# A retention and SwiGLU kernel: the first 740 of its listed steps in another order

## The chip, the cores and the metric

The kernel runs on one core of one Trainium2 chip. The metric is the device time of one execution in microseconds (us). Five engines work side by side, each in the order of its own program: TensorE (PE; its weight loads, PEld, are listed apart), VectorE (DVE), ScalarE (ACT), GpSimd (POOL) and SyncE (SP), which here only starts transfers (DMAs).

## The reference

Two blocks follow one another, all in float32. The first is a recurrent retention over 768 positions for 4 batches and 8 heads of 64 columns. The second is a SwiGLU feed-forward block on its result.

```python
gamma = 1.0 - 2.0 ** (-5.0 - np.arange(H))          # B, H, S, D = 4, 8, 768, 64
for t in range(S):
    state = gamma[None, :, None, None] * state + np.einsum('bhd,bhe->bhde', k[:, :, t], v[:, :, t])
    y[:, :, t] = 1.0 / np.sqrt(D) * np.einsum('bhd,bhde->bhe', q[:, :, t], state)
x = y.transpose(0, 2, 1, 3).reshape(3072, 512)
g = x @ w_gate                                       # 512 x 1536
val = x @ w_val                                      # 512 x 1536
out = (g / (1 + np.exp(-g)) * val) @ w_out           # 1536 x 512
```

## The kernel before

*Products.* A float32 operand of a large product is split into three terms of the shorter type fp32r, and three (or, for two split operands, several) products are summed in a PSUM bank. The first term is a rounding by ScalarE (lines 1129, 1138), the second a remainder by VectorE (lines 418, 1132), the third a remainder by GpSimd (lines 1135, 1141) or VectorE (line 1145). So every operand passes through three engines before TensorE can use it.

*Tiling.* The 3072 tokens are taken in four segments of 768 tokens, six chunks of 128 each. A segment has an up stage (gate and value products for 12 blocks `f` of 128 of the 1536 columns, silu, product of the two) and a down stage (`D`: for each `f` and each of the six chunks, three matmuls into one of six banks). The up stages of segments 1 to 3 use a scheme with seven products per block (line 1230). The retention of the next segment runs between the steps of the down stage.

*Order.* The string `PLAN` lists the names of all steps; `run()` goes through it and executes each step, so that each engine's instructions, and the transfers in SyncE's queue, stand in the order of the list.

```python
for key in PLAN.split():
    if key in events:
        events.pop(key)[2]()
    else:
        do(key)
```

A step can hold work of one engine or a transfer, and an engine does its steps strictly in that order, whichever of them is ready first. A transfer is issued by SyncE in list order and, before it is issued, waits for its target buffer to be free.

*Names of steps in segment 0.* A name is a letter, a number and, after the colon, a part.

- `A` loads parts of the decay tables; `l c:0` to `l c:3` load chunk `c` (keys, queries, values and the keys in rows: four transfers of 256 KB); `P` loads the chunks' data for segment 1 (line 928).
- `s c` scores (matmuls L651, masked by VectorE L657); `m c` mix of the scores with the values (L742); `o` the part of the older state (L728); `t` the new state (matmuls L713, VectorE L718); `r` transposes keys (L692); `k` and `q` scale keys and queries on GpSimd, `K` and `Q` on VectorE, `E` on ScalarE; `g` lets a state decay (ScalarE), `I` makes a unit matrix.
- `x c:0` to `x c:2` split a chunk's result into three terms: `x4:1` is the remainder term of chunk 4 (VectorE L418).
- `U`, `V` bring a weight block's raw 64-bit words; `a`, `b`, `c` (ScalarE L553, L556, L559), `S` and `C` (VectorE L566, L574; GpSimd L576 for the blocks 12 to 17 of the down weights) turn them into float32; `T` makes sums and differences of weight terms for the scheme of the later segments (VectorE L418); `Z` stores the converted weights for the later segments; `n f:0` to `n f:5` make the three terms of gate and value weights.
- `p f:j` and `v f:j`, for `f` = 0 and 1, are the gate and value products for two of the six chunks (L1075, 12 matmuls of 256 columns each); `G f:i` and `W f:i`, for `f` from 2, are those products for three chunks (L1057); `u`/`i` is the silu, `y`/`j` the product of the two (VectorE L1086, L463).

*Names in the down stage and in the retention of segment 1.* `0/W f` loads a block of the down weights and `0/d f.0` to `0/d f.2` split it (ScalarE L1138, GpSimd L1141, VectorE L1145). `0/h f.0` to `0/h f.2` split the block's activations. `0/D f.tok` are the three matmuls for one chunk of tokens (L1301). `1/sc p` are scores (matmuls L825), `1/dec p.i` masks them (VectorE L956), `1/q`, `1/k` scale queries and keys, `1/A p`, `1/B p` and `1/C p` are three mixes (matmuls L825), `1/y...` copies of their results, `1/x...` splits of the sum. `0/e` and `0/o` end a chunk's output and store it.

`down` of line 1295 shows what a `D` step asks of the others:

```python
for n, (g, a) in enumerate(own):
    nc.tensor.matmul(o, hs[g][:, a, ds(i * TH + u * P, P)], wo[g][:, a, cols],
                     start=n == 0 and (f == 0 or final),
                     stop=f == NF - 1 and a == 2, skip_group_check=True)
```

The three matmuls read the terms `a` = 0, 1, 2 of the activations `hs` (steps `0/h`) and of the weights `wo` (steps `0/d`), one after the other, and `o` is a bank that another product may still hold.

Of the kernel before, what the change touches and what calls it, by code (L numbers as in the profile page):

```python
# [25 lines left out]
L = 3  # L26
# [65 lines left out]
    0/D2.5 1/sc1 0/D2.0 0/d4.0 1/was1.0 0/D2.4 0/d4.1 0/D3.4 1/l6 1/dec1.1 0/h5.2 1/dec1.0 0/D2.2
    1/x0.2.0 0/D3.1 1/q1.1 0/d4.2 0/W5 0/D3.5 1/x0.1.0 0/h6.0 1/k1.0 0/Z3 1/sum0.3 1/k1.1 1/sum0.2
    1/x0.2.1 0/D4.5 0/D3.2 0/D3.3 0/D3.0 1/q1.0 0/Z4 0/h6.1 0/D4.0 0/D4.4 1/x0.1.2 1/x0.1.1 1/A1
    1/x0.0.0 0/d5.0 1/x0.2.2 1/y1.00 0/h6.2 1/y1.06 1/x0.0.2 1/new1.0 0/D4.2 0/d5.1 0/d5.2 0/D4.3 0/D4.1
    1/y1.07 1/y1.01 0/W6 0/h7.0 1/B1 1/x0.0.1 1/y1.04 1/y1.12 0/h7.1 1/l9 0/d6.0 0/D5.4 0/h8.0
    0/d6.1 1/y1.02 0/D5.3 0/D5.2 0/W7 0/h8.1 1/y1.05 0/d6.2 1/l8 1/l11 0/Z5 1/y1.03 1/was1.1
# [30 lines left out]
    1/p8.4 1/w9.0.1 2/l1 0/o5 0/o4 1/u5.7 2/k0.0 2/cv3 1/u7.8 1/w9.1.2 1/w9.0.2 1/L11 2/l0
    1/u7.9 1/p9.0 1/u8.1 1/w8.2.2 1/u8.5 1/u8.6 1/p9.1 1/w10.1.0 1/w10.2.0 1/w10.0.0 1/u9.0 1/u7.2 1/w9.2.1
    1/w10.1.1 1/w10.1.2 1/w10.0.1 2/l4 1/w10.0.2 1/p9.3 1/p9.2 1/u9.4 1/p8.6 1/u9.3 1/p9.4 1/p9.5 1/u8.2  # L130
    1/u8.8 1/u8.9 1/p10.0 1/u9.5 2/sc0 1/w9.2.2 1/u9.6 1/u9.1 1/p10.1 2/l5 2/l6 1/u8.7 1/w11.1.0
    1/w11.0.0 1/w11.0.1 1/w11.1.1 1/u10.0 1/w11.2.0 1/p10.2 1/p9.6 1/W0 2/l2 2/k0.1 1/u10.3 1/p10.3 1/u9.8
    1/u9.9 1/p10.4 1/u10.4 1/p10.5 1/h0.0 1/u10.1 2/dec0.0 1/u7.7 1/u9.2 1/u10.2 1/w10.2.1 1/u10.5 1/w11.1.2
# [1369 lines left out]
```

## Time and profile before

| what | value |
| --- | --- |
| runs (us) | 639.65, 640.67, 639.59; median 639.65 |
| profiled execution: span | 641.7 us |
| granted clock of TensorE, mean | 0.997 |
| TensorE busy | 630.8 us (98%), 5601 matmuls |
| weight loads | 581.7 us (91%) |
| VectorE busy | 506.9 us (79%), 764 instructions |
| ScalarE busy | 396.6 us (62%), 845 instructions |
| GpSimd busy | 173.2 us (27%), 117 instructions |
| moved by DMA | 143.03 MB, mean 223 GB/s |

The reordered steps end near 196 us of the span; from there to the end both kernels have the same list. The busy times say how much of the span an engine worked; the waits and the order of time, quoted below, say which engine kept another one waiting. In a row of the order of time stand the start, the length, the engine and line, the operation, output and inputs with their shapes, a count where equal instructions stand in one row, and in brackets the idle time before it with what ended it. The times of all views are from the one profiled execution.

### The profile page before, as it was taken

What the parts mean: (1) busy time and instruction counts of PE and PEld (TensorE: products, weight loads), DVE (VectorE), ACT (ScalarE), POOL (GpSimd) and SP (SyncE); (2) the same over time, 40 slices, a digit from 0 to 9 for tenths busy, and PEclk for the clock granted to TensorE, in tenths of its full rate; (3) what the DMA queues carried; (4) which work ended last, traced back from release to release, by engine and by line L of the source; (5) the groups of instructions that cost most, each with busy time, mean ns of one, the idle gap of its engine ahead of it and who ended that gap; (6) DMA issues with size and microseconds to landing.
All of it is one profiled execution on the core that took longest, in us unless ns stands there. A gap on an engine that the chain in (4) does not pass through costs nothing.

```text
span 641.7 us, 14131 instructions
## 1 busy us (share of the span) xinstructions
PE 630.8 (98%) x5601; PEld 581.7 (91%) x5601; DVE 506.9 (79%) x764; ACT 396.6 (62%) x845; POOL 173.2 (27%) x117
## 2 busy tenths in 40 slices
PE   7999999999999999999899999999999999999997
PEld 6899999987789999997788999998888999999886
DVE  4998788899898889887489777978778888877551
ACT  4786897677866665667376664756764655564220
POOL 0544455544423531210001343340002014232000
PEclk9999999999999999999899999999999999999999
DMA  9899998689788443688783435577785345304764
GB/s 319 289 353 311 372 333 274 259 323 305 281 278 305 140 157 115 214 263 239 204 312 130 179 115 206 173 203 229 229 290 196 113 149 189 128 13 140 230 212 149
DMA packets 57747, 143.03 MB, mean 223 GB/s; under 512 B 5840, under 2 KB 28368, under 8 KB 57680
## 3 DMA queue, kind: packets, MB, share of 16 engines
q1 hardware_dynamic: 57104, 141.33, 64.5%
q8 instruction: 44, 0.72, 0.5%
q10 hardware_dynamic: 576, 0.79, 0.3%
q14 instruction: 23, 0.19, 0.1%
HBM read 112.21 MB, written 29.88 MB: 221 GB/s over the span
## 4 chain that ended last, share of the span: by engine, by line
PE 94%; DMA 5%; ACT 1%; SPq 1%; issue 0%; DVE 0%; ACTq 0%
PE bank L1230 41%; PE bank L1301 30%; PE bank L1057 13%; PE bank L825 5%; PE bank L1075 3%; DMA oitem<-wdnt 2%; DMA hT<-in_v_n_dram 2%; PE bank L742 1%; DMA hT<-in_q_t_dram 1%; PE bank L728 0%; SPq L820 0%; PE bank L713 0%; PE bank L651 0%; ACT gitem L1129 0%; ACT local L871 0%
## 5 line engine op out<-in xcount | busy, mean ns | idle before, releaser
L1301 PE MATMUL bank<-oitem,gitem 128*128 128x512 f32 (+1 forms) x873 | 205.9, 393 | 3.0 <-DMA oitem<-wdnt 2.9
L1301 PEld LDWEIGHTS bank<-oitem,gitem 128*128 128x128 f32 x873 | 161.9, 189 | 38.1 <-DMA oitem<-wdnt 3.5
L1230 PE MATMUL bank<-xa,gitem 128*128 128x384 f32 x864 | 160.6, 334 | 0.0
L1230 PEld LDWEIGHTS bank<-xa,gitem 128*128 128x128 f32 x864 | 150.6, 188 | 0.1
L1135 POOL TENSOR_TENSOR gitem<-gitem 128x768 fp32r<-128x768 f32 x36 | 72.1, 2007 | 185.0 <-DVE gitem L1132 165.7
L1135 POOL TENSOR_TENSOR oitem<-oitem 128x512 fp32r<-128x512 f32 (+1 forms) x48 | 52.8, 1105 | 168.1 <-DVE oitem L1132 148.0
L418 DVE SCALAR_TENSOR_TENSOR gitem<-gitem 128x768 fp32r<-128x768 f32 x84 | 86.6, 1041 | 1.7 <-DVE gitem L1132 0.5
L1057 PE MATMUL bank<-xa,oitem 128*128 128x384 f32 x480 | 84.2, 335 | 0.0
L1230 PE MATMUL bank<-xb,gitem 128*128 128x384 f32 x432 | 83.7, 335 | 0.0
L1057 PEld LDWEIGHTS bank<-xa,oitem 128*128 128x128 f32 x480 | 83.0, 188 | 0.2
L1230 PEld LDWEIGHTS bank<-xb,gitem 128*128 128x128 f32 x432 | 75.8, 188 | 0.4
L1129 ACT ACTIVATE gitem<-loads 128x768 fp32r<-128x768 f32 x72 | 59.1, 842 | 25.7 <-PE bank L1230 16.9
L1132 DVE SCALAR_TENSOR_TENSOR gitem<-gitem,loads 128x768 fp32r<-128x768 f32 x72 | 70.5, 991 | 3.4 <-ACT gitem L1129 3.3
L1132 DVE SCALAR_TENSOR_TENSOR gitem<-gitem,hT 128x768 fp32r<-128x768 f32 x48 | 46.2, 965 | 28.0 <-ACT gitem L1129 24.1
L1129 ACT ACTIVATE gitem<-hT 128x768 fp32r<-128x768 f32 x48 | 40.2, 844 | 43.7 <-PE bank L1301 35.3
L1230 PE MATMUL bank<-xb,oitem 128*128 128x384 f32 x216 | 43.0, 335 | 0.0
L1230 PEld LDWEIGHTS bank<-xb,oitem 128*128 128x128 f32 x216 | 38.0, 188 | 0.0
L1246 ACT COPY tmp<-bank 128x384 f32<-128x384 f32 x36 | 17.3, 480 | 27.0 <-PE bank L1230 22.9
L1247 DVE TENSOR_TENSOR hT<-bank,tmp 128x384 f32<-128x384 f32 x36 | 20.0, 554 | 16.5 <-PE bank L1230 16.4
L1245 ACT COPY tmp<-bank 128x384 f32<-128x384 f32 x36 | 17.2, 479 | 24.8 <-PE bank L1230 17.1
L1249 DVE TENSOR_TENSOR hT<-hT,bank 128x384 f32<-128x384 f32 x36 | 19.7, 550 | 13.4 <-ACT bank L1249 13.2
L1247 ACT COPY tmp<-bank 128x384 f32<-128x384 f32 x36 | 17.3, 481 | 16.5 <-PE bank L1230 11.9
(152 smaller groups left out, 807.2 us busy)
## 6 DMA issues: line engine op xcount, KB each, us to landing
loads<-wup SPq DMA_DIRECT2D x36, 896.0 KB, 5.4
oitem<-wdnt SPq DMA_DIRECT2D x33, 768.0 KB, 4.7
wdnt<-oitem SPq DMA_DIRECT2D x12, 768.0 KB, 5.8
wup<-first SPq DMA_DIRECT2D x9, 896.0 KB, 6.9
rawp<-in_w_gate_dram SPq DMA_DIRECT2D x12, 512.0 KB, 7.3
rawp<-in_w_val_dram SPq DMA_DIRECT2D x12, 512.0 KB, 6.6
rawp<-in_w_out_dram SPq DMA_DIRECT2D x12, 512.0 KB, 5.8
out_dram<-chunk_x SPq DMA_DIRECT2D x21, 256.0 KB, 4.7
```

The costliest lines, as they stand in the source:

```text
L418: stt(o, x, 1.0, y, op0=mul, op1=op)
L825: nc.tensor.matmul(o, a, b, start=start, stop=True, skip_group_check=True)
L1057: nc.tensor.matmul(o, w[:, a, ts(b, P)], X0[:, a, i, NC - 1 - b], start=a == b == 0, stop=a == 2 and b == NC - 1, skip_group_check=True)
L1075: nc.tensor.matmul(o, w[:, a, ts(b, P)], X0[:, a, :, NC - 1 - b, ts(j, P)], start=a == b == 0, stop=a == 2 and b == NC - 1, skip_group_che ...
L1129: act(o[0], x, AF.Copy, scale=CUT / FAR)
L1132: stt(o[1], f32(o[0]), -FAR, x, op0=mul, op1=add)
L1135: op(o[2], f32(o[0]), f32(o[1]), op=add)
L1230: nc.tensor.matmul(o, w[:, a, k], x[:, a, KH - 1 - k], start=start and a == k == 0, stop=a == 2 and k == KH - 1, skip_group_check=True)
L1246: lambda: act(gate, c11, AF.Silu, scale=ONE), lambda: copy(u2, x),
L1247: lambda: copy(p5, wb), lambda: tt(h1, x, p5, op=add),
L1249: lambda: act(x, x, AF.Silu, scale=ONE), lambda: tt(h1, h1, x, op=mul))
L1301: nc.tensor.matmul(o, hs[g][:, a, ds(i * TH + u * P, P)], wo[g][:, a, cols], start=n == 0 and (f == 0 or final), stop=f == NF - 1 and a == ...
```

## The change

The first 740 entries of `PLAN` stand in a new order. No step is added, left out or altered, and buffers and transfers are the same; what follows the step `1/w1.0.1 0/e0 0/o0` is the old list (broken into other lines in the file). Of the diff these are the start, the places around the transfers `P0` to `P2`, `l4:3` and `l5:3`, the passage into the down stage, and the places of the mixes.

```diff
-    A0 I0 l0:0 l1:0 A2 A1 U0:0 s0 a0:1 r1 l0:2 s1 b0:1
-    A4 A3 l2:1 l2:0 r0 m0 K0 S0:1 c0:1 l1:2 x0:1 t0 s2
-    E1 l3:0 l3:1 m1 l2:3 C0:1 g2 V0:0 a0:0 Q2 n0:0 b0:0 l2:2
-    x1:2 s3 x1:1 n0:1 l4:1 l4:0 l3:2 t1 S0:0 k2 x0:2 q3 c0:0
-    C0:0 o2 U1:1 m2 o3 n0:3 s4 m3 a1:1 n0:4 x2:1 l5:1 l3:3
-    b1:1 x2:2 x3:1 S1:1 t2 n0:2 p0:0 q4 a1:0 x3:2 c1:1 n0:5 k3
-    C1:1 g3 b1:0 n1:0 v0:0 l5:0 U2:3 s5 S1:0 t3 c1:0 C1:0 l5:2
-    p0:1 n1:1 u0:0 u0:1 T0:0 q5 v0:1 a2 l4:2 b2 y0:1 o5 y0:0
-    o4 n1:3 S2 n1:2 m5 T0:1 n1:4 c2 m4 n1:5 x5:2 p1:0 l5:3
-    x5:1 p1:1 u1:0 C2 v1:0 U3:1 T0:2 x4:2 T1:0 U12:0 a3 v1:1 y1:0
-    x4:1 T1:1 L b3 p0:2 a12 c12 n2:0 S3 u1:1 T1:2 b12 u0:2
...
-    n5:1 j3:1 Z3 T4:1 n5:3 i4:0 n5:2 T4:2 S6 W4:0 b13 c6 i4:1
-    G5:0 j4:1 S7 C13 j4:0 G5:1 n6:2 a8 n6:3 P2 n6:4 i5:1 c14
-    n7:4 W6:1 b14 g4 n7:2 G7:0 i6:1 W6:0 P0 c8 S14 C8 Z6
-    C14 h2 a9 b9 G7:1 j6:1 n7:5 S9 n8:0 c15 n8:3 j6:0 k5
...
-    P1 n11:4 T11:0 T11:1 1/was0.0 T11:2 n11:1 W10:0 Z11 c17 n11:2 n11:5 b17
-    0/h0.1 0/W0 G11:1 0/h1.0 G11:0 j10:0 0/d0.0 h1 0/h0.2 1/sc0 j10:1 i11:0 0/h1.1
-    0/W1 S17 0/d1.0 i11:1 0/d0.1 1/l3 C17 T10:0 1/dec0.0 W11:0 0/d1.1 0/d0.2 W11:1
-    0/h2.0 j11:0 0/D0.2 j11:1 1/k0.0 1/l4 1/dec0.1 1/q0.0 0/D0.1 1/q0.1 0/D0.4 1/k0.1 1/l5
-    0/D0.0 0/h2.1 0/d1.2 0/h1.2 0/h4.0 0/W2 0/Z0 1/A0 1/y0.06 1/new0.0 0/h4.1 1/y0.01 0/D0.5
...
-    0/D5.5 1/C1 0/d7.0 1/y1.16 0/d7.1 0/D6.5 0/D5.0 1/y1.17 1/y1.15 1/new1.1 0/h7.2 1/y1.14 1/y1.11
...
-    0/D11.0 1/x2.0.0 0/D11.3 0/D10.5 0/D11.4 1/w0.0.1 0/D11.2 1/w0.0.2 1/w1.0.0 1/x2.1.1 1/x2.0.1 0/Z10 1/w1.0.1
+    A0 I0 l0:0 l1:0 A1 A2 U0:0 l0:2 A4 l2:1 s0 a0:1 r0 s1 r1 l2:0 K0 l3:0 l1:2 b0:1 S0:1 m0 c0:1
+    x0:1 C0:1 t0 A3 E1 s2 m1 Q2 n0:0 l3:1 x0:2 V0:0 l4:0 l3:2 t1 a0:0 s3 n0:1 b0:0 o2 S0:0 q3 l2:2
+    l4:1 c0:0 l2:3 U1:1 x1:2 x1:1 o3 C0:0 m3 l3:3 n0:2 l5:0 x3:1 m2 k2 l5:1 x2:2 n0:3 p0:0 g2 n0:4
+    x2:1 g3 a1:1 b1:1 s4 x3:2 S1:1 c1:1 C1:1 n0:5 t2 a1:0 v0:0 b1:0 S1:0 p0:1 k3 u0:0 u0:1 q4 c1:0
+    v0:1 U2:3 l4:2 t3 n1:0 C1:0 L n1:3 s5 l5:2 a2 q5 l4:3 o5 n1:1 n1:4 o4 b2 S2 U3:1 y0:1 m4 m5 x4:2
+    U12:0 n1:2 y0:0 p1:0 c2 p1:1 T0:0 x5:1 C2 U4:3 T0:1 n1:5 u1:0 a3 v1:0 h0 v1:1 b3 x4:1 x5:2 y1:0
+    p0:2 T0:2 a12 S3 u1:1 u0:2 n2:0 T1:0 c3 v0:2 y1:1 n2:1 C3 n2:3 p1:2 v1:2 u1:2 Z0 b12 c12 U13:1
...
+    G9:0 c10 C15 0/h0.0 n9:4 j7:1 C10 n9:5 t4 l5:3 T9:0 U16:3 a11 j8:0 W8:1 G9:1 i9:0 Z15 b11 j8:1
+    P1 n10:0 k5 n10:3 c16 n10:4 0/h0.1 i9:1 a16 T8:1 t5 b16 n10:1 P0 S11 S16 W9:0 n10:2 W9:1 n10:5
+    G10:0 j9:0 j9:1 c11 G10:1 C11 W10:0 T9:1 1/was0.0 T8:2 n11:0 n11:3 i10:0 n11:4 1/sc0 T11:0 C16
+    i10:1 T11:1 T10:0 U17:2 P2 T11:2 0/h1.0 0/h1.1 W10:1 Z16 n11:1 Z8 a17 b17 Z11 n11:2 c17 T9:2
+    1/q0.1 S17 G11:0 n11:5 j10:0 C17 j10:1 0/W0 G11:1 W11:0 0/d0.0 W11:1 0/d0.1 1/dec0.0 i11:0
+    1/q0.0 0/h0.2 1/l5 j11:0 1/dec0.1 0/d0.2 i11:1 0/D0.4 0/D0.2 1/l3 0/h2.0 0/h2.1 0/W1 1/k0.0
+    0/D0.1 Z9 0/h4.0 0/Z0 0/W2 j11:1 0/d1.0 0/d1.1 0/D0.5 1/k0.1 0/h1.2 0/D0.3 1/l11 0/D0.0 T10:1
...
+    0/d6.2 1/y1.05 0/W8 1/y1.02 1/y1.03 1/l9 1/C1 0/D6.4 0/Z6 0/D6.0 0/h7.2 0/d7.0 0/D6.1 1/l10
...
+    0/D9.2 1/y2.00 0/D9.0 0/D9.4 1/x1.0.0 1/new2.0 0/W11 1/B2 1/w0.0.0 0/Z9 1/y2.02 0/d11.0 1/x1.2.2
+    1/C2 0/d10.1 0/d10.2 0/D9.5 0/h10.2 0/D9.3 1/y2.10 1/y2.16 0/h11.2 1/x1.0.2 1/y2.11 0/D10.4
...
+    1/x2.1.2 1/x2.0.0 1/w1.0.0 0/D11.1 1/x2.0.1 0/D11.2 0/Z11 0/Z10 1/w1.0.1 0/e0 0/o0 1/x2.0.2
```

In the new list `1/B1` is the last matmul step before `1/C1`, and `1/B2` the last before `1/C2`; in the old one down steps stand between them.

More of the change, by code (lines that the diff above doesn't have):

```diff
@@ L92 @@
[L92 to L97, printed above, removed]
@@ L128 @@
[L128 to L132, printed above, removed]
@@ new lines @@
+    U10:2 G8:0 n9:1 a15 T7:2 n9:2 n8:4 b15 n9:3 a10 U11:1 b10 i8:0 i8:1 T8:0 n8:5 S15 S10 Z7 W8:0
+    G9:0 c10 C15 0/h0.0 n9:4 j7:1 C10 n9:5 t4 l5:3 T9:0 U16:3 a11 j8:0 W8:1 G9:1 i9:0 Z15 b11 j8:1
[3 more added lines that the diff above has]
+    1/q0.1 S17 G11:0 n11:5 j10:0 C17 j10:1 0/W0 G11:1 W11:0 0/d0.0 W11:1 0/d0.1 1/dec0.0 i11:0
@@ new lines @@
+    2/w10.0.0 2/p8.6 2/u8.6 2/u9.0 2/p9.2 2/p9.3 2/w10.1.1 2/w10.1.2 2/w10.0.1 2/w10.0.2 3/l1 3/sc0
+    3/l6 3/l5 3/l4 2/u9.3 2/p9.4 2/w10.2.0 2/u9.4 2/p9.5 2/u8.8 2/w11.1.0 2/u9.5 2/w10.2.1 2/p9.1
+    2/p9.6 3/dec0.1 2/u9.6 2/p10.3 2/w11.1.1 2/w11.1.2 2/u8.9 2/w11.0.0 2/w11.2.0 2/u7.2 2/u9.1
+    2/p10.0 2/p10.1 2/w11.0.1 2/u9.8 2/u8.2 2/u7.7 2/W0 3/l2 2/u9.9 2/w11.2.1 3/l10 3/l11 2/u10.0
+    2/u10.1 2/u10.4 2/p10.2 2/u10.3 2/p10.5 2/u9.2 3/dec0.0 2/w11.0.2 2/w11.2.2 2/p11.0 2/p10.4
+    2/h0.0 2/u10.6 2/p11.3 3/q0.0 2/h0.1 2/u10.5 3/q0.1 2/u11.0 2/p11.2 2/h1.0 2/h1.1 3/l9 3/k0.1
@@ L235 @@
+    3/h11.0 3/W8 2/o4 3/D8.2 3/D8.4 3/D8.1 3/D8.5 3/D8.3 3/D8.0 3/h9.1 3/h9.2 3/W9 3/h11.1 3/h10.1
+    3/h10.2 3/h11.2 3/W10 3/W11 3/D9.0 3/D9.3 3/early 3/D9.1 3/D9.4 3/D9.5 3/D10.4 3/D10.5 3/D11.4
+    3/D11.5 3/e4 3/o4 3/e5 3/o5 3/D10.0 3/D11.0 3/e0 3/o0 3/D10.3 3/D11.3 3/e3 3/o3 3/D10.1 3/D11.1
+    3/e1 3/o1 3/D11.2 3/e2 3/o2
 """
```

286 lines of the change are left out of this document (142 added, 144 removed).

## The prediction

> **What bounds the kernel now.** I read the page first, then the waits of TensorE, then the windows, then the order of time in the first 25 us and around 130 us.
>
> ```profile
> span 641.7 us, 14131 instructions
> PE 630.8 (98%) x5601; PEld 581.7 (91%) x5601; DVE 506.9 (79%) x764; ACT 396.6 (62%) x845; POOL 173.2 (27%) x117
> PE 94%; DMA 5%; ACT 1%; SPq 1%; issue 0%; DVE 0%; ACTq 0%
> ```
>
> TensorE (PE) is busy 98% of the span and carries 94% of the chain that ends last. The span is 2.05 us above the median of the three runs (639.65), so I work out differences on the span and subtract them from the median.
>
> ```profile
> PE bank L1301 <- DMA oitem<-wdnt: 2.9, 1, 2.9
> PE bank L651 <- DMA hT<-in_k_t_dram: 1.7, 2, 1.1
> PE bank L742 <- DMA hT<-in_v_n_dram: 1.4, 2, 0.9
> PE bank L651 <- DVE tmp L657: 0.4, 1, 0.4
> ```
>
> These are nearly all the waits TensorE has. The first row lies at 304 us, after the reordered stretch; the other three lie in the first 20 us, 1.1 of `L651` ahead of its very first matmul.
>
> ```profile
> 0.00:20.00 20.00, 15.50 (x206) 13.41 (x208) 11.85 (x20) 9.52 (x25) 3.62 (x7) 1.00 0.94 328
> 20.00:40.00 20.00, 20.00 (x246) 18.84 (x242) 18.47 (x32) 16.54 (x28) 8.27 (x7) 1.00 0.89 301
> 120.00:140.00 20.00, 20.00 (x294) 17.85 (x293) 18.27 (x25) 15.99 (x39) 11.59 (x7) 1.00 0.72 262
> 140.00:160.00 20.00, 20.00 (x271) 15.87 (x273) 18.87 (x30) 15.92 (x50) 7.32 (x4) 1.00 0.91 316
> ```
>
> The columns are TensorE, weight loads, VectorE (DVE), ScalarE (ACT), GpSimd (POOL), clock, DMA share, GB/s. From 20 us on TensorE has no gap, and VectorE runs right behind it: 18.3 to 18.9 of 20 us. So the 740 steps, which end near 196 us, can win only the gaps of the first 20 us and a little of what TensorE loses when it changes from one kind of work to another. They can lose wherever VectorE falls behind.
>
> **The change part by part.** No instruction is added or removed; every term is a move.
>
> *The start.* The waits of TensorE, in order of time, are these.
>
> ```profile
> 9.90 1.09 PE L742 MATMUL bank<-tmp,hT 128*64 128x128 f32 x16 [0.54 <-DMA hT<-in_v_n_dram]
> 11.99 1.16 PE L651 MATMUL bank<-hT 64*128 64x128 f32 x16 [0.51 <-DMA hT<-in_k_t_dram]
> 14.53 1.16 PE L651 MATMUL bank<-hT 64*128 64x128 f32 x16 [0.36 <-DVE tmp L657]
> 18.24 1.09 PE L742 MATMUL bank<-tmp,hT 128*64 128x128 f32 x16 [0.86 <-DMA hT<-in_v_n_dram]
> 22.87 3.13 PE L1075 MATMUL bank<-xa,oitem 128*128 128x256 f32 x24
> 34.49 11.78 PE L1075 MATMUL bank<-xa,oitem 128*128 128x256 f32 x96
> 37.84 0.68 DVE L418 SCALAR_TENSOR_TENSOR first<-first 128x512 f32<-128x512 f32 x1
> 39.16 0.42 DVE L1086 TENSOR_TENSOR hT<-bank,tmp 128x256 f32<-128x256 f32 x1 [0.65 <-ACT bank L556]
> 39.50 0.68 DVE L418 SCALAR_TENSOR_TENSOR xa<-xa,bank 128x512 fp32r<-128x512 f32 x1
> ```
>
> They are `m0` (0.54), `s2` (0.51), `s3` (0.36) and `m2` (0.86). `m0` waits for `l0:2`, which keeps its place in the transfer queue: 0.54 stays. For `s2`, table part `A3` goes behind `l2:1` and `l2:0`; one 256 KB transfer at the 328 GB/s of the first window is 0.8 us, so the 0.51 goes. `s3` waits for VectorE to empty its banks; now `t1` (about 0.65) runs first, and the 0.36 goes. `m2` waits for `l2:2`; now `o3` and `m3` run before it (about 2 us), and the 0.86 goes. That is 1.73 at most.
>
> VectorE gives part of it back. At `p0:2` (34.49 plus half of 11.78, so 40.4) TensorE needs `x4:1`, which ended at 39.50 + 0.68 = 40.18. In the new order `T1:0` (0.68), `y1:0` (0.42), `x5:2` (0.68 like `x4:1`) and `T0:2` (0.42 like `y1:0`) stand behind `x4:1` instead of ahead of it: 2.2 us less work. But TensorE now asks for `x5:2` as well, and `S1:1` and `C1:1` stand side by side, so that VectorE waits about 0.7 us while ScalarE does `c1:1` between them. Followed by hand with the durations of before, `x4:1` ends near 40.0 and `x5:2` near 40.6, where TensorE without any wait would be at 40.4 - 1.73 = 38.7. Of the twelve matmuls of `p0:2` (1.47 us) the first four read only what `x4:0` wrote, and `x5:2` is read by the last four: it can start at 39.6, 0.8 early. Every other step followed by hand can be late too, none can be much earlier: bounds 0.3 and 0.9, and I take 0.6, near the VectorE rows rather than the 1.73.
>
> *Stage 0 and the transfers.* In the SP queue `P2`, `P0` and `l5:3` go back past the weight loads `U9` to `U11` and the stores `Z5` to `Z7`, `P1` and `l4:3` forward.
>
> ```profile
> loads<-in_k_t_dram SPq DMA_DIRECT2D x6, 256.0 KB, 4.0
> 126.96 1.09 PE bank L825 x64
> 105.56 1.29 POOL L1135 TENSOR_TENSOR oitem<-oitem 128x512 fp32r<-128x512 f32 x1
> 109.43 0.69 PE L713 MATMUL bank<-chunk_x 128*64 128x64 f32 x16
> ```
>
> The first reader of `P0` and `P1` is `1/sc0`, at 126.96 before and some 6 us earlier now. They are issued behind `Z15`, near 107 us, and land 4 us later: 9 us of cover. `l5:3` is read by `k5`, which now stands on GpSimd behind `n9:5` (the row at 105.56) and takes about 1.05; it would end near 107.9, and `t5` (109.43, or 108.8 with the gain) needs it: 0.9 us of cover, the thinnest place of stage 0. I cost these moves at nothing; if GpSimd is late there, each microsecond beyond 0.9 is one of TensorE's. The many swaps of `G` and `W` halves are between equal steps: nothing.
>
> *Fewer changes of work in the down stage.* `1/B1` and `1/C1`, and `1/B2` and `1/C2`, now stand side by side, so that twelve runs of down steps become ten.
>
> ```profile
> 132.41 2.97 PE bank L1301 x12
> 185.52 10.43 PE bank L1301 x45
> ```
>
> A matmul costs 0.248 in a short run and 0.232 in a long one: 12 x 0.016 = 0.19 for a run. Two runs fewer are 0.4; I take 0.35, bounds 0 and 0.4.
>
> *The entrance of the down stage.* Now `0/D0.4` is first, ahead of `0/D0.2` and `0/D0.1`. It writes the banks that `1/dec0.1` reads and needs `0/d0.2`, and both are VectorE's.
>
> ```profile
> 126.52 1.29 POOL L1141 TENSOR_TENSOR oitem<-oitem 128x512 fp32r<-128x512 f32 x1 [2.01 <-ACT oitem L1138]
> 127.93 2.81 POOL L576 TENSOR_TENSOR first<-first,rawp 128x1024 int32<-128x1024 int32 x1
> 130.69 1.76 POOL L1141 TENSOR_TENSOR oitem<-oitem 128x512 fp32r<-128x512 f32 x1
> 122.90 0.56 DVE L463 TENSOR_TENSOR hT<-bank,tmp 128x384 f32<-128x384 f32 x1 [0.80 <-PE bank L1057]
> 123.37 1.95 DVE L418 SCALAR_TENSOR_TENSOR gitem<-gitem 128x768 fp32r<-128x768 f32 x1
> 125.72 0.94 DVE L1132 SCALAR_TENSOR_TENSOR gitem<-gitem,hT 128x768 fp32r<-128x768 f32 x1
> 127.78 0.68 DVE L418 SCALAR_TENSOR_TENSOR first<-first 128x512 f32<-128x512 f32 x1
> 128.38 0.68 DVE L956 TENSOR_TENSOR tmp<-bank,local 128x512 f32<-128x512 f32 x1
> 128.98 2.31 DVE L1145 SCALAR_TENSOR_TENSOR oitem<-oitem 128x512 fp32r<-128x512 f32 x1
> 132.25 3.13 PE L1301 MATMUL bank<-oitem,gitem 128*128 128x512 f32 x12
> ```
>
> Two VectorE steps here took far longer than their kind: `0/h0.2` 1.95 for 0.94, `0/d0.2` 2.31 for 0.68. Both read all operands from SBUF and lie beside a GpSimd step (`C17` is the 2.81). Together they lost 2.64 us. In the new order VectorE does, between the end of `S17` and that of `0/d0.2`: `j10:0`, `j10:1`, `j11:0` (0.55 each), `1/dec0.0`, `1/q0.0`, `1/dec0.1`, `0/d0.2` (0.68 each) and `0/h0.2` (0.94), 5.3 us. `S17` ends near 124.7 by hand. TensorE, 0.6 early, reaches `0/D0.4` at 131.65, and reads the last part of `0/d0.2` 0.45 later. The spare time is 132.1 - 124.7 - 5.3 = 2.1. With the 2.64 of before the wait is 0.5; bounds 0 and 2.0, when `C17` and `0/d0.1` (2.81 + 1.29 = 4.1) are waited out in full. I take 0.6: the queue order of GpSimd puts `C17` and `0/d0.1` right where `1/q0.0` and `0/h0.2` stand.
>
> [...]
>
> *Behind it.* `0/W2` now stands in the SP queue behind `0/Z0`, which waits for the same `0/d0.2`; `0/D2.0`, its reader, stands about ten steps of TensorE later, which hides it. After 196 us the order is the old one; the wait of 2.9 us there follows from TensorE's own progress and stays.
>
> *Sum.* -0.6 - 0.35 + 0.6 = -0.35, so 639.65 - 0.35 = 639.3.
>
> The start has a second reading.
>
> ```profile
> q8 instruction: 1, 0.02, 2.3%
> first<-in_q_t_dram SPq DMA_DIRECT2D x1, 256.0 KB, 9.3
> ```
>
> Between 15 and 18 us one packet of code passes, and the transfer issued just before took 9.3 us to land, where its kind takes 4 to 5: this is a late transfer, and the 0.86 of `m2` hangs on it. [...]
>
> **The rivals.**
>
> *Slower: VectorE is late at the entrance of the down stage.* Beyond 2.1 us of standing between `S17` and `0/d0.2`, each microsecond is one of TensorE's, and VectorE, at 18.9 of the next 20 us, has little to catch up with. With 4.1 the wait is 2.0: -0.95 + 2.0 = +1.05, 640.7. A second such meeting has the price of a row above, 1.0 to 1.6, and gives 641.7 to 642.3. For it: the two long rows, and GpSimd busy 11.59 of 20. Against it: these meetings exist already and TensorE passes them without a gap.
>
> *Faster: the start pays more.* If `x4:1` and `x5:2` come in time, 1.5 of the 1.73 pass; with the 0.35 and no wait at 132 that is -1.85, 637.8. With half of the wait, 638.1. For it: 2.2 us less VectorE work ahead of `x4:1`. Against it: VectorE is busy 18.47 of 20 us there.
>
> *The order does nothing.* A wait takes the place of each wait removed and the runs cost as before: 639.65. It lies within the forecast's band.
>
> **How the numbers follow.** A measurement of this kernel can tell about 0.2%, 1.28 us, from no change. The forecast, with the order that does nothing, lies inside: 0.44. Slower by more than 1.28 needs the entrance at its upper bound and one more meeting, or some place that I did not follow among 740 steps, each with little slack: 0.35. Faster by more needs nearly the whole start: 0.21. The range leaves out one in ten at each end: low 638.0 (just above the full gain), high 642.0 (one more meeting on top of the entrance's upper bound, without its worst).
>
> **What would show it.** Right: the waits of `L651` and `L742` below 20 us behind DMAs fall from 3.1 to about 1.7, the 0.4 behind VectorE goes; `L1075` starts near 20.5; TensorE waits for VectorE at the first `L1301` by about 0.6; ten runs of `L1301` to 196 us. Wrong: a wait over 1 us of TensorE anywhere from 40 to 196 us, or the 2.9 at 304 us changed.

## The result and the profile after

The changed kernel took 644.82 us (median of four, 643.54 to 646.41), the kernel before 639.62 (median of four): a ratio of 1.0073 with a 95% interval of 1.0047 to 1.0099. It is 5.2 us slower; 639.3 was forecast, within 638.0 to 642.0.

Line numbers are 7 lower in the changed kernel, since its list is broken into fewer lines: L818 is L825 of before, L1157 is L1164, L1294 is L1301. In the experiments with another list they are 15 lower (L810, L1149, L1286); `before_again` and `w1_filled` have the numbers of before.

The head of the page after:

```profile
span 643.6 us, 14132 instructions
PE 630.9 (98%) x5601; PEld 582.7 (91%) x5601; DVE 506.8 (79%) x764; ACT 396.6 (62%) x845; POOL 172.0 (27%) x117
```

The busy times are those of before, so the loss is idle time. The windows of after show where; the columns are those of the prediction's windows.

```profile
0.00:20.00 20.00, 17.62 (x206) 15.65 (x208) 10.50 (x19) 8.30 (x21) 2.05 (x6) 1.00 0.96 327
120.00:140.00 20.00, 20.00 (x269) 18.06 (x271) 18.51 (x24) 12.44 (x30) 11.05 (x7) 1.00 0.88 303
140.00:160.00 20.00, 18.00 (x221) 14.37 (x212) 14.56 (x24) 15.76 (x50) 6.19 (x6) 1.00 0.94 324
160.00:180.00 20.00, 17.71 (x313) 14.27 (x311) 15.87 (x24) 13.70 (x39) 4.92 (x4) 1.00 0.85 292
180.00:200.00 20.00, 18.04 (x229) 14.57 (x226) 17.98 (x26) 10.74 (x25) 7.26 (x4) 1.00 0.72 241
```

TensorE, which had no gap there before, is idle for 2.0, 2.3 and 2.0 us in the last three windows. VectorE, which had been busy 18.87 of 20 us from 140 to 160, is busy 14.56: it is idle as well. The order of time of TensorE in the changed kernel, only rows with a wait, names the places.

```profile
5.75 2.08 PE L644 MATMUL bank<-hT 64*128 64x128 f32 x16 [0.93 <-DMA hT<-in_k_t_dram]
12.55 0.69 PE L706 MATMUL bank<-hT 128*64 128x64 f32 x16 [0.36 <-DVE hT L665]
142.50 0.46 PE L818 MATMUL bank<-loads,states 64*64 64x64 f32 x16 [0.99 <-ACT chunk_x L1157]
152.22 1.16 PE L818 MATMUL bank<-loads 64*64 64x64 f32 x64 [1.00 <-ACT chunk_x L1157]
167.31 0.46 PE L818 MATMUL bank<-loads,states 64*64 64x64 f32 x16 [1.13 <-DVE states L1025]
169.63 0.46 PE L818 MATMUL bank<-loads,states 64*64 64x64 f32 x16 [1.17 <-ACT chunk_x L1157]
185.25 0.69 PE L818 MATMUL bank<-tmp,loads 64*64 64x64 f32 x32 [1.58 <-DVE tmp L949]
191.06 0.46 PE L818 MATMUL bank<-loads,states 64*64 64x64 f32 x16 [0.38 <-ACT chunk_x L1157]
```

The six rows of `L818` are, in order, the steps `1/C0`, `1/sc1`, `1/B1`, `1/C1`, `1/A2` and `1/C2`. They sum to 6.25 us, all inside the down stage of segment 0. The waits of `s2`, `s3` and `m2` in the start are gone as forecast, one of 0.36 for VectorE at the first state step (`t0`, `L706`) is new, and there is none at the entrance of the down stage, at 132.

The profile of before that the prediction read was not a usual execution. A second profile of the same kernel (experiment 1) has a span of 637.3, and its step times equal the first one's within 0.5 us up to 304 us; there the first lost 4.4 us: the 2.87 of the wait and, behind it, matmuls at half rate. The windows of that first profile:

```profile
304.00:306.00 2.00, 0.05 (x1) 0.00 (x0) 2.00 (x4) 1.42 (x5) 0.00 (x0) 1.00 0.93 332
308.00:310.00 2.00, 2.00 (x7) 1.58 (x6) 2.00 (x4) 1.32 (x5) 0.00 (x0) 0.55 1.01 270
```

In the last but two column the granted clock is 0.55. Against the second profile the account closes: the first product behind the down stage (`1/p0.0`) starts at 195.86 before and at 201.78 after, 5.92 later, and `p1:0`, where the start ends, at 34.46 and 34.45. So all 5.9 arise in between: 6.25 of waits, less 0.3. From the first down step to `1/p0.0` TensorE is busy 63.4 us, where it was 63.8 before.

VectorE's own order of time (only waits over 0.4 us, 134 to 192 us), first in the second profile of before, then in the changed kernel:

```profile
144.67 0.97 DVE L1032 TENSOR_TENSOR states<-states,bank 128x256 f32<-128x256 f32 x2 [0.43 <-PE bank L825]
163.06 1.42 DVE L1132 SCALAR_TENSOR_TENSOR gitem<-gitem,hT 128x768 fp32r<-128x768 f32 x1 [1.50 <-ACT gitem L1129]
166.55 0.42 DVE L1032 TENSOR_TENSOR states<-states,bank 128x256 f32<-128x256 f32 x1 [0.93 <-ACT chunk_x L1164]
```

```profile
138.24 0.75 DVE L1025 TENSOR_TENSOR states<-states,bank 128x256 f32<-128x256 f32 x2 [0.95 <-ACT chunk_x L1157]
146.47 0.75 DVE L1025 TENSOR_TENSOR states<-states,bank 128x256 f32<-128x256 f32 x2 [2.69 <-ACT chunk_x L1157]
154.22 0.69 DVE L1138 SCALAR_TENSOR_TENSOR oitem<-oitem 128x512 fp32r<-128x512 f32 x1 [2.71 <-POOL oitem L1134]
171.63 0.69 DVE L1138 SCALAR_TENSOR_TENSOR oitem<-oitem 128x512 fp32r<-128x512 f32 x1 [1.26 <-POOL oitem L1134]
174.87 0.76 DVE L1025 TENSOR_TENSOR states<-states,bank 128x256 f32<-128x256 f32 x2 [2.54 <-ACT chunk_x L1157]
```

These are `1/new0.0`, `1/new0.1`, `0/d4.2`, `0/d7.2` and `1/new1.1`. In these rows VectorE stands 10.2 us in sum with the next step of its list not ready, against 2.9 before.

### The profile page after: what moved, and what is told of

Its sections match the earlier page's. It is cut to its first block, busy times and chain, and to the rows that moved or that the text cites. A ratio compares the mean times of both kernels' runs of the same rounds, so it can differ in the third digit from the quotient of the medians.

```text
span 643.6 us, 14132 instructions
## 1 busy us (share of the span) xinstructions
PE 630.9 (98%) x5601; PEld 582.7 (91%) x5601; DVE 506.8 (79%) x764; ACT 396.6 (62%) x845; POOL 172.0 (27%) x117
## 4 chain that ended last, share of the span: by engine, by line
PE 92%; DVE 3%; DMA 2%; ACT 1%; issue 1%; SPq 0%
PE bank L1223 41%; PE bank L1294 27%; PE bank L1050 13%; PE bank L818 5%; PE bank L1068 3%; PE bank L644 1%; DMA oitem<-wdnt 1%; PE bank L735 1%; DMA hT<-in_k_t_dram 1%; ACT chunk_x L1157 1%; PE bank L706 1%; PE bank L721 1%; DVE gitem L1125 1%; DMA loads<-in_k_n_dram 1%; DVE loads L411 0%
## 5 line engine op out<-in xcount | busy, mean ns | idle before, releaser
L1294 PE MATMUL bank<-oitem,gitem 128*128 128x512 f32 (+1 forms) x873 | 203.6, 391 | 0.4 <-DMA oitem<-wdnt 0.4
L1294 PEld LDWEIGHTS bank<-oitem,gitem 128*128 128x128 f32 x873 | 160.8, 188 | 34.9 <-DMA oitem<-wdnt 1.0
L411 DVE SCALAR_TENSOR_TENSOR gitem<-gitem 128x768 fp32r<-128x768 f32 x84 | 88.4, 1063 | 1.3
L1239 ACT COPY tmp<-bank 128x384 f32<-128x384 f32 x36 | 17.2, 478 | 27.0 <-PE bank L1223 20.8
L1238 ACT COPY tmp<-bank 128x384 f32<-128x384 f32 x36 | 17.2, 478 | 24.1 <-PE bank L1223 16.4
L1134 POOL TENSOR_TENSOR oitem<-oitem 128x512 fp32r<-128x512 f32 x12 | 18.2, 1520 | 37.2 <-ACT oitem L1131 37.2
```

The costliest lines, as they stand in the source:

```text
L411: stt(o, x, 1.0, y, op0=mul, op1=op)
L1134: op(o[1], f32(o[0]), x, op=sub)
```

## The experiments

Each was run beside the kernel before on the same chip; differences are between the medians of one session, with the ratio over all runs and its interval. Single executions of one order scatter by 2 to 6 us. The changed kernel itself was not run again: its 5.2 (3.0 to 6.3 by its interval) comes from its own four runs, so a difference between it and a version of it is known to some 2 us only.

**1. The kernel before once more** (no edit, one profile).

> The kernel before, unchanged, profiled once more, to see whether the 2.9 us wait of L1301 for a transfer at 304 us belongs to every execution. The changed kernel's profile has a span of 643.6 for a time of 645.44, 1.84 apart; the medians 639.62 and 644.82 are 5.2 apart, the two spans only 1.9. Theory: the wait was an accident of the one profiled execution; here it is absent or under 0.5, and the span is about 638 to 639. Rival: it stands here again with 2 to 3 us at the same place, and the span is 641 to 642; then the spans and not the medians mislead for another reason.

Time 639.12, span 637.3, no wait of `L1301` over 0.3 near 304. The theory held: span and time stand 1.8 apart in both kernels, so the first profile's 641.7 means a time near 643.5, above all runs shown. One other execution of 24 came to 643.28, with the mean clock of the first profile, 0.997.

**2. Which part of the order costs.** The list is cut at the entrance of the down stage.

```diff
-all entries in the new order
+e1_head: entries 1 to 442 of the new list (to i11:1), the others as in the old list
+e2_tail: entries 1 to 444 of the old list (to j11:0), the others as in the new list
+e4_start: the new list to p0:2, the others as in the old list
```

> The new order up to the entrance of the down stage (its first 442 steps, up to i11:1), and behind it all other steps in the old order. Theory: the loss lies only in the down stage, in six waits of TensorE at L825 (6.24 us in sum in the changed kernel) that come from how the down steps, the y copies and the state updates are mixed there; the start gains 2.1 us (its waits fall from 3.41 to 1.29) and stage 0 is neutral. So 2.1 faster than before, 637.5, and no wait over 0.5 from 130 to 196 us. Rival: the new head brings VectorE or the transfers late to the down stage, so that any order behind it waits; then the same waits stand here too, and the time is at or above before, 640 to 645.

> The old order up to the entrance of the down stage (its first 444 steps), and behind it all other steps in the new order. Theory: the whole loss and none of the gain: the waits at L825 of about 6.2 us come again, the start keeps its 3.4 us of waits, so about 6 slower than before, 645 to 646.5. Rival (the head is to blame): no slower than before by more than 1 us, 639 to 640.6.

> The new order only for the start (up to p0:2, some 40 us), and all other steps in the old order. Theory: the gain of 2.1 us comes from the first 20 us alone and lasts to the end: 637.5, the same as with the new order up to the down stage. Rival: the gain at the start is handed back behind it, where VectorE (18.5 of 20 us) has to follow a faster TensorE; then a wait of TensorE for VectorE of 1 us or more between 40 and 100 us, and 639 to 640.

`e2_tail` came out 7.9 slower (1.0116, 1.0099 to 1.0134), `e1_head` 0.8 slower (1.0008, 0.9996 to 1.0020), `e4_start` 0.8 slower (1.0007, 0.9996 to 1.0018). The loss lies in the new order of the down stage. The gain of 2.1 did not come in either; each has a wait of its own at the cut (`1/A0` 1.1 inside it, `v1:2` 0.58). In `e2_tail` the six waits are back (6.5 in sum), and with them one at the first down step:

```profile
134.01 4.36 PE L1286 MATMUL bank<-oitem,gitem 128*128 128x512 f32 x18 [1.34 <-DVE tmp L941]
```

This is `0/D0.4`, the first down step, waiting for `1/dec0.1`: the wait that was forecast, 1.34 in place of 0.6, in a kernel whose stage 0 is the old one.

**3. Taking the six waits away.** Steps of the changed kernel are moved.

```diff
 f1_copy
-1/x0.2.0 0/D2.2 1/sum0.1 0/W5 1/y0.13
+1/y0.13 1/x0.2.0 0/D2.2 1/sum0.1 0/W5
 f2_cover
-1/C0 ... 0/D1.2 ... 0/D1.5   1/C1 0/D6.4 0/Z6 0/D6.0   1/C2 ... 0/D9.5 ... 0/D9.3
+0/D1.2 0/D1.5 ... 1/C0       0/D6.4 0/D6.0 1/C1 0/Z6   0/D9.5 0/D9.3 1/C2
 f3_vector
-0/h6.2 0/D5.0 1/new1.0       1/dec2.1 1/q2.0 0/h11.1 0/D8.2 0/Z8 1/dec2.0
+1/new1.0 0/h6.2 0/D5.0       1/dec2.1 1/dec2.0 1/q2.0 0/h11.1 0/D8.2 0/Z8
 f4_all: all of these
```

> The changed kernel with one step moved: the copy 1/y0.13 (ScalarE) ahead of 1/x0.2.0 in the list, behind which it stood while that waited for the store Z10. Theory (each of the six waits at L825 has a cause of its own): the wait of 1/sc1 of 1.0 us goes, the other five stay, and the time is 1.0 below the changed kernel, 643.8. Rival (VectorE and ScalarE are short in the whole stage): what sc1 no longer waits is waited at 1/B1, 1/C1 or 1/A2, and the time stays at 644.6 to 645.

> The changed kernel with two down steps each put between a B mix and its C mix: 0/D1.2 and 0/D1.5 ahead of 1/C0, 0/D6.4 and 0/D6.0 ahead of 1/C1, 0/D9.5 and 0/D9.3 ahead of 1/C2. Theory: C overwrites what the eight copies behind B still read, 1.4 us of down steps cover them, and the waits of 1/C0, 1/C1 and 1/C2 (0.99, 1.17, 0.38) go: 2.5 below the changed kernel, 642.3, with the rest of the waits as they were. Rival (VectorE short): later state updates make B1 and A2 wait longer, and less than half is gained, 643.6 to 644.8.

> The changed kernel with two VectorE steps moved ahead: 1/new1.0 ahead of 0/h6.2, and 1/dec2.0 directly behind 1/dec2.1 (ahead of 1/q2.0 and 0/h11.1). Theory: 1/B1 and 1/A2 wait for these alone (1.13 and 1.58), so 2.7 below the changed kernel, 642.1. Rival: the steps that now come later on VectorE (0/h6.2, 1/q2.0, 0/h11.1) are needed as soon, by 0/D6.4 or by the mix itself, and less than half is gained, 643.5 to 644.8.

> The changed kernel with the moves of the three others together (nine steps of 2368 in another place). Theory: all six waits at L825 go, 6.2 below the changed kernel, 638.6, level with the kernel before or up to 0.5 below it. Rival (short engines): waits of TensorE between 136 and 192 us still sum to over 3 us, and the time is above 641.

Against before: `f1_copy` +4.9, `f2_cover` +5.5, `f3_vector` +3.3, `f4_all` +2.9 (1.0043, 1.0026 to 1.0060), where the changed kernel had +5.2. `f2_cover` and `f4_all` were expected at +2.7 and -1.0: three waits taken away bring nothing that can be measured, all six bring 2.3. So the theory of six separate causes fell. `f1_copy`, expected 1.0 below the changed kernel, can't tell, as that is within the noise. `f3_vector`, which moves two steps of VectorE and no matmul, brought 1.9 of the 2.7 expected, and in the same session it lies 2.2 below `f2_cover`. In it the waits of `1/B1` and `1/A2` are gone, the four behind ScalarE stay (3.8), and one at `0/D9.2` has come:

```profile
185.04 1.88 PE L1286 MATMUL bank<-oitem,gitem 128*128 128x512 f32 x7 [0.57 <-DVE oitem L1130]
```

In `f2_cover` the waits of the three `C` mixes are gone, and others have come:

```profile
150.59 1.21 PE L1286 MATMUL bank<-oitem,gitem 128*128 128x512 f32 x4 [1.16 <-DVE oitem L1130]
177.23 1.19 PE L1286 MATMUL bank<-oitem,gitem 128*128 128x512 f32 x4 [0.35 <-DVE oitem L1130]
185.43 0.69 PE L810 MATMUL bank<-tmp,loads 64*64 64x64 f32 x32 [2.25 <-DVE tmp L941]
```

Each is behind VectorE: `0/D3.5` for `0/d3.2`, `0/D8.3` for `0/d8.2`, and `1/A2`, which waited 1.58, for `1/dec2.0`. In `f4_all` 6.25 became 2.73, all of it for VectorE's third terms:

```profile
150.32 1.20 PE L1286 MATMUL bank<-oitem,gitem 128*128 128x512 f32 x4 [1.13 <-DVE oitem L1130]
175.55 1.20 PE L1286 MATMUL bank<-oitem,gitem 128*128 128x512 f32 x4 [0.34 <-DVE oitem L1130]
185.42 1.89 PE L1286 MATMUL bank<-oitem,gitem 128*128 128x512 f32 x7 [1.26 <-DVE oitem L1130]
```

**4. VectorE at the head of its queue.** Five steps are moved, none of them a matmul.

```diff
 g1_vqueue (changed kernel), g2_both (the same in f4_all)
+1/was0.1 directly behind 1/y0.02     1/new0.1 directly behind 1/C0
+0/d4.0 directly ahead of 1/x0.2.0
+1/was1.1 directly ahead of 1/y1.17   1/new1.1 directly behind 0/h8.2
```

> The changed kernel with five steps moved so that VectorE does not stand at the head of its queue: 1/was0.1 (ScalarE) behind 1/y0.02 and 1/new0.1 (VectorE) behind 1/C0, 0/d4.0 (ScalarE) ahead of 1/x0.2.0, 1/was1.1 ahead of 1/y1.17 and 1/new1.1 behind 0/h8.2. Theory now: VectorE's own idle time (2.7 at new0.1, 2.7 at 0/d4.2, 1.3 at 0/d7.2, 2.6 at new1.1, about 9 us between 134 and 192 us, against under 3 before) is the root, and TensorE's waits are where it shows. So VectorE's idle time falls below 4 us, 1/B1 and 1/A2 wait less, and although the waits of C0, sc1 and C1 (3.2) stay, the time falls by 2 or more, to 642.8 or less. Rival: TensorE's waits come from the ScalarE copies alone; then nothing is gained, 644.3 to 645.2.

> The changed kernel with these five moves and the nine of the run that took all six waits at L825 away and came to 642.4. Theory: there the waits came back at 0/D3.5, 0/D8.3 and 0/D9.2 for splits that VectorE had late (1.1, 0.3, 1.3); with VectorE no longer standing, the first two go as well: 640.4 or less, within 1 of before. Rival: the new order of the down stage needs more of ScalarE or GpSimd in some place too, waits of over 2 us come at yet other steps, and the time stays at 642 or above.

`g1_vqueue` came to +2.6 (1.0033, 1.0021 to 1.0046), half of the loss, with every matmul in the order of the changed kernel. The waits of `1/B1` and `1/A2`, whose steps were not touched, are gone; those of the copies stay:

```profile
142.95 0.46 PE L810 MATMUL bank<-loads,states 64*64 64x64 f32 x16 [0.96 <-ACT chunk_x L1149]
152.70 1.16 PE L810 MATMUL bank<-loads 64*64 64x64 f32 x64 [0.84 <-ACT chunk_x L1149]
168.82 0.46 PE L810 MATMUL bank<-loads,states 64*64 64x64 f32 x16 [1.18 <-ACT chunk_x L1149]
188.60 0.46 PE L810 MATMUL bank<-loads,states 64*64 64x64 f32 x16 [0.38 <-ACT chunk_x L1149]
```

VectorE's busy time from 134 to 192 us says the same, first the changed kernel, then `g1_vqueue`, then before (second profile):

```profile
134.00:192.00 58.00, 51.75 (x839) 41.28 (x838) 47.48 (x67) 37.52 (x106) 18.06 (x14) 1.00 0.84 283
```

```profile
134.00:192.00 58.00, 54.59 (x850) 43.42 (x849) 51.11 (x68) 40.07 (x115) 21.08 (x14) 1.00 0.85 293
```

```profile
134.00:192.00 58.00, 58.00 (x865) 46.18 (x865) 53.98 (x77) 43.24 (x124) 20.48 (x13) 1.00 0.85 294
```

VectorE (third pair) works 47.48, 51.11 and 53.98 of 58 us. Its idle time fell by 3.6, not to under 4 as expected: it still stood 2.6 at `1/new1.1` and 2.0 at `0/h5.1`. `g2_both` came to +1.4 (1.0024, 1.0013 to 1.0035): 3.8 of the 5.2 are back. Of the waits of `f4_all` those at `0/D8.3` and `0/D9.2` went, that at `0/D3.5` stayed (1.08) and one at `0/D7.4` came (0.48), so this expectation was missed narrowly in the sum (at most 1 above before was expected) and in the place.

The idle time of both engines from 134 to 192 us (58 less the busy time of the same view) can be set beside the time of these kernels:

| kernel | TensorE idle | VectorE idle | median less before |
| --- | --- | --- | --- |
| before (second profile) | 0.0 | 4.0 | 0 |
| `v1_split` (below) | 0.7 | 4.9 | +1.1 |
| `g2_both` | 1.6 | 7.4 | +1.4 |
| `g1_vqueue` | 3.4 | 6.9 | +2.6 |
| `f4_all` | 2.7 | 11.1 | +2.9 |
| `f3_vector` | 4.4 | 11.5 | +3.3 |
| `f1_copy` | 5.6 | 11.0 | +4.9 |
| changed kernel | 6.2 | 10.5 | +5.2 |
| `f2_cover` | 5.2 | 10.4 | +5.5 |

The time follows TensorE's idle time within 1.1 us. It does not follow VectorE's: `f3_vector` and `f4_all` came 1.9 and 2.3 below the changed kernel although VectorE stood no less. The row of `f4_all`:

```profile
134.00:192.00 58.00, 55.28 (x850) 42.75 (x849) 46.90 (x68) 38.72 (x111) 22.38 (x14) 1.00 0.83 283
```

So `g1_vqueue` shows that the order of VectorE's queue is behind a part of the loss; that its idle time as a whole sets the loss is not shown.

A standing put into the old order:

```diff
 v1_split (kernel before)
+0/d4.0 and 0/d4.1 directly behind 1/x0.2.0
```

> The kernel before with one pair of steps moved into a place like that of the changed order: 0/d4.0 (ScalarE) and 0/d4.1 (GpSimd) behind 1/x0.2.0, which waits for the store Z10. Theory (VectorE is the engine that sets the end of the down stage of segment 0, TensorE's waits only show it): VectorE stands for 0/d4.2 for 1 to 2 us, TensorE waits up to that much for a later split or score, and the time is 0.6 to 1.6 above before. Rival: the wait is hidden, as 0/D4 comes late enough and TensorE sets the pace: level with before within 0.4.

It is 1.1 slower than before (1.0019, 1.0007 to 1.0030). VectorE stood 1.42 at `0/d4.2`, and TensorE waited at `0/D4.5`: its third matmul started 1.10 us behind its second, where 0.23 is usual. Of these 0.87 the profile's row names 0.71. As `0/d4.2` is itself what `0/D4.5` reads, this gives the price of one late split; it does not show that standing costs as much where no matmul waits for that step.

```profile
152.12 1.76 DVE L1130 SCALAR_TENSOR_TENSOR oitem<-oitem 128x512 fp32r<-128x512 f32 x1 [1.42 <-POOL oitem L1126]
153.94 3.92 PE L1286 MATMUL bank<-oitem,gitem 128*128 128x512 f32 x16 [0.71 <-DVE oitem L1130]
```

**5. The start.** The first two have the new order up to the down stage, the seam of `e1_head` mended; the next two have it to `G2:1` only.

```diff
 b1_start (e1_head with)
+1/l3 1/k0.0 behind i11:1, 1/k0.1 0/h2.0 behind 0/d1.0, 0/h2.1 behind 0/h1.2
 s1_start: the new list to G2:1, the others as in the old list
 b2_filled (b1_start), s2_filled (s1_start), w1_filled (before), s3_filled (s1_start, l1:2 ahead of l3:0)
-    warm_up(5, 16)
+    warm_up(27, 16)
```

> The new order up to the entrance of the down stage and the old one behind it, as in the run that came to 639.8, with the seam mended: there 1/A0 lost 1.1 us inside, waiting for 1/k0.1; now the load 1/l3 and the steps 1/k0.0 and 1/k0.1 come earlier on SP and ScalarE, and 0/h2.0 and 0/h2.1 behind them. Theory: the gain of the new start (1.3 us where TensorE's first matmuls run at full rate, 0.1 where they run at half rate, as in about half of the profiles so far) reaches the end: median 0.3 to 1.3 below before. Rival: the gain is lost again elsewhere in the down stage, level with before or slower.

> The same with 22 more of the small warm-up matmuls (16 columns) behind the existing ones, so that TensorE has no gap of about 1 us ahead of the first scores. Theory: the half rate of the first 3.5 us in about half of the profiles comes from that gap; without it the first scores always take 1.1 and not 2.0 us, and the time is 1.2 to 1.5 below before and less scattered. Rival: the rate is settled by something else, or the added matmuls hold the scores up: no faster than the same order without them.

> The new order only for the start, cut later than before (up to G2:1, some 48 us), so that the late step 1 of VectorE at the earlier cut (y1:1, 0.58) is not in it; the rest in the old order. Theory: p1:0 starts at 33.2 to 33.4 where TensorE's first matmuls run at full rate and at 34.4 to 34.7 where they run at half rate for 3.5 us (34.46 with the old start at full rate); no wait from there to 200 us. So 1.2 faster in some executions and level in the others: median 0.3 to 1.0 below before. Rival: the new start brings later steps into new waits even with a clean seam: level with before or slower by up to 1.

> The same with 22 more of the small warm-up matmuls, so that TensorE has no gap ahead of the first scores. Theory: full rate always, p1:0 near 33.4, and 0.9 to 1.3 faster than before. Rival: the filler or the earlier start costs what it saves (a transfer is then the next to be late, as l1:2 was in the profile of the other filled kernel, 1.24): no faster than without it.

> The kernel before with only the 22 more small warm-up matmuls. Theory: the filler gives TensorE full rate from the first scores on, but the old start waits for transfers anyway (its p1:0 stood at 34.73 at half rate and 34.46 at full rate), so the time is within 0.3 of before, and p1:0 starts at 34.2 to 34.5. So the 1.06 of the filled new start comes from the order and the rate together. Rival: the filler alone gives 0.7 or more.

> The new start with the filler, and the load l1:2 ahead of l3:0 in the transfer queue, since m1 waited 1.24 for l1:2 in both profiles of filled kernels. Theory: l1:2 lands 0.7 to 0.8 earlier, the wait of m1 falls to about 0.5 and s3 still finds l3:0 and l3:1 in time; p1:0 starts near 32.7, 0.7 ahead of the kernel without this move, and the time is 1.5 to 1.8 below before. Rival: what m1 gains s3 or m2 waits for, and p1:0 stays at 33.2 to 33.5, 1 below before.

| kernel | median less before | ratio, interval | `p1:0` starts at |
| --- | --- | --- | --- |
| `b1_start` | +1.6 | 1.0030, 1.0014 to 1.0045 | 33.26 |
| `b2_filled` | +1.9 | 1.0041, 1.0021 to 1.0060 | 33.60 |
| `s1_start` | -0.1 | 0.9999, 0.9987 to 1.0011 | 34.59 |
| `s2_filled` | -1.1 | 0.9989, 0.9977 to 1.0001 | 33.43 |
| `w1_filled` | +0.9 | 1.0017, 0.9998 to 1.0037 | 34.59 |
| `s3_filled` | +0.4 | 1.0005, 0.9993 to 1.0018 | 33.31 |

The mending in `b1_start` was a miss: `1/B0` and `1/sc1` then wait 0.64 and 0.83 for VectorE and ScalarE. With a clean seam the new start is level with before; with the filler it reaches `p1:0` a microsecond earlier than before, and no time shows that beyond its interval. Part of it is given back near 80 us, under the old order of stage 0, as in `s2_filled`, where `G6:0` waits for a silu:

```profile
79.07 25.26 PE L1042 MATMUL bank<-xa,oitem 128*128 128x384 f32 x144 [0.53 <-ACT tmp L448]
```

In `s3_filled` the wait of `m1` fell to 0.35 and `s3` waited 0.51 instead, as its rival had it. The filler alone (`w1_filled`) gains nothing; five of its twelve executions show a mean clock of 0.996 or 0.997, and the other seven have a median 0.1 above before. No version was shown to be faster than the kernel before.

## Why the prediction was wrong

Both signs of being wrong that the prediction named came: three waits of TensorE of over 1 us between 40 and 196 us, and the 2.9 at 304 us gone.

**The step that failed** is the one headed "Fewer changes of work in the down stage", the only term that the prediction gave to that stage behind its entrance: -0.35. The price itself was right: there are ten runs of down steps in place of twelve, and TensorE's busy time there fell by 0.4. But the term held no waits, and the new order brought six, 6.25 us in sum. Putting `1/C1` behind `1/B1` and `1/C2` behind `1/B2` took away the four down steps that had stood between each pair; between `1/B0` and `1/C0` one of six is left. A `C` mix overwrites the bank parts that eight copies of ScalarE (0.26 each) have to empty first, and some of those wait for `B`. Behind `1/B0` seven copies, six of them of that part, stand in one row that ends at 142.44, and `1/C0` starts at 142.50:

```profile
140.66 1.78 ACT L1157 COPY chunk_x<-bank 64x128 f32<-64x128 f32 x7 [0.51 <-PE bank L818]
```

The prediction did not name the work that had hidden these copies, and stopped following VectorE and ScalarE by hand at 132 us, where their lists in the new order begin to differ most. `1/B1` and `1/A2`, 2.7 of the 6.25, waited for VectorE.

**The size** is that of TensorE's waits in this stage, and VectorE is behind a part of them: moving steps of VectorE ahead gave 1.9 back (`f3_vector`), and making it stand less, with a few steps of ScalarE, gave 2.6 (`g1_vqueue`), with the order of the matmuls untouched. Covering the copies alone gave nothing, since other steps then waited for VectorE (`f2_cover`). All the moves together gave 3.8 of 5.2; the waits that then remain, 1.6 us, were not taken away by any run. The rival "VectorE is late" named this engine and the price of about one for one. It put the place at the entrance and the cause in VectorE's meetings with GpSimd; the place was the whole stage, and the cause, as far as it was shown, the order of its queue.

**The entrance:** 0.6 forecast, 0 measured. The meeting came, and worse than before: `0/h0.2`, 0.94 alone, took 3.18 beside `C17`. The rows are VectorE's and GpSimd's in the changed kernel.

```profile
126.84 3.18 DVE L411 SCALAR_TENSOR_TENSOR gitem<-gitem 128x768 fp32r<-128x768 f32 x1
126.33 2.87 POOL L569 TENSOR_TENSOR first<-first,rawp 128x1024 int32<-128x1024 int32 x1
```

It ended 0.82 behind `C17`, near the 0.94 that it takes alone; that it stood until GpSimd was through is a reading of these two rows. TensorE passed at 132.31 without a gap all the same: `S17` had ended at 123.91, 0.8 earlier than by hand, and `0/d0.2` was ready at 132.38, 0.4 ahead of the third matmul of `0/D0.4`. So the spare time was mis-sized and not the meeting, and the pass was a narrow one; with the old stage 0 ahead of the same entrance it waited 1.34.

**The start:** the waits of `s2`, `s3` and `m2` went as forecast, and `p0:2` was not held by VectorE: in `e1_head` it began at 39.06, where 39.6 was the earliest by the prediction. The term of 0.6 was mis-sized for another reason: `p1:0` began 1.0 to 1.5 us earlier than before (the four profiles of the new start whose first scores ran at full rate) or within 0.3 of it (the seven at half rate; see the last section). That this gain would last to the end was not shown.

**Stage 0:** the moves costed at nothing cost nothing; `k5`, `t5` and the `P` loads caused no wait.

**The basis:** "the wait of 2.9 us there follows from TensorE's own progress and stays" was false. It was an accident of that execution, absent from the second profile, and the 2.05 between span and median, with every listed run below, was the sign. Left in, it would have hidden most of the loss: the two spans differ by 1.9 only.

**The range** ended 2.7 us above the forecast: 1.4 for the entrance and 1.3 for one more meeting. The chance of 0.35 for a slower time did name "some place that I did not follow", and that is what came; but 1.3 us was too little for some 300 steps in a stage where the second engine is busy 93%.

## What to carry to other kernels

Where the second engine is nearly as busy as the first, follow its list through the whole reordered stage and not only to the stage's entrance: a wait of the first engine that is taken away can come back at another step (1.16 at `0/D3.5` in `f2_cover`), and moving steps of the second one forward can pay without moving any of the first's (1.9 us back in `f3_vector`). The first engine's idle time, summed over the stage, told the loss within 1.1 us; the second engine's did not. Before two steps that share a bank are put side by side, list what must empty the bank between them. Compare a profile's span with the listed runs before using it, and take it again if it lies above all of them.

## What the runs showed of the hardware

TensorE's first scores took 2.08 us in nine of the fifteen profiles without the filler and 1.16 in six, whatever the order: pairs of matmuls stood 0.21 us apart in the one case (the changed kernel) and 0.11 in the other (the first profile of before). The rows are of the changed kernel (above, at 5.75) and, here, of `e1_head`:

```profile
5.91 1.16 PE L636 MATMUL bank<-hT 64*128 64x128 f32 x16 [1.09 <-DMA hT<-in_k_t_dram]
```

The column of the granted clock shows 1.00 in both cases. But that column is 1.00 wherever the trace has no clock record, and the first record, of the full clock, begins at 10.10 us in the changed kernel and at 4.41 in the first profile of before. The full-size warm-up matmuls, from 1.1 to 4.0 us, stood 0.21 us apart in both. So in the changed kernel the half rate was there ahead of the gap of about 1 us before the scores, and the gap did not bring it. In all nine profiles the half rate ended soon: four transposes (`r`) took 1.11 us near 8 us, and the next four, which start at 10.0 to 10.8 us, took 0.66.

TensorE's wait ahead of the scores was 0.86 to 1.12 us in the nine and 1.05 to 1.37 in the six. In the four profiles with warm-up matmuls in that gap the first scores took 1.16 to 1.38 us. What ends the half rate, and whether the gap puts that off, is not shown: four profiles are few beside six of fifteen.

In the first profile of before the wait of 2.87 us at 304 was followed by half a clock again: TensorE went on at 306.92, the clock record is half from 308.20 to 311.61, 3.41 us, the matmuls in it stand 0.43 us apart and those behind it 0.23, and this cost another 1.5 us behind the wait. The second profile, without the wait, shows 1.00 from 308 to 310. That the wait brought the half clock is the author's reading of this one case.
